# Early staging of the first batch and an even gMLP pace in a block-sparse attention + gMLP kernel

## The chip, the cores and the metric

The kernel runs on one core of one Trainium2 chip. The metric is the device time of one execution in microseconds (us); lower is better. The runs of the kernel before are summed up by their median. Engines are named as in the profile: PE (TensorE matmuls), PEld (TensorE weight loads), DVE (VectorE), ACT (ScalarE), POOL (GpSimd) and SP (SyncE, which here only issues DMAs). L12 is line 12 of the kernel before.

## What is computed

Two stages in one launch. First, attention with a block mask: batch 4, 8 heads, 768 positions, head dimension 64, blocks of 32, so 24 x 24 blocks. A block pair is visible if the blocks are neighbours, if one is the first or last block, or if it is one of three sampled blocks of that row. Second, a gMLP with a spatial gate on the attention output of all heads side by side (512 features).

```python
scores = (1/8) * q @ k.T ;  scores = where(mask, scores, -1e9)
x = softmax(scores) @ v                      # heads side by side: (4, 768, 512)
h = relu(x @ w_in)                           # 512 -> 1024
u, v = h[..., :512], h[..., 512:]
v_n = (v - mean(v)) / sqrt(var(v) + 1e-6)    # over features
v_s = w_spatial @ v_n + b_spatial            # over positions, 768 x 768
out = (u * v_s) @ w_out                      # 512 -> 512
```

## The kernel before, in words

Heads are taken in pairs: pair p is heads 2p and 2p+1 of the running count, four pairs a batch, sixteen in all (NP). For each pair q, k and v are loaded in float32 into staging tiles (`st_tile`, L89; two buffers for each of q, k, v), cast to bf16 (`cast_qk` L104, `cast_v` L112, `prepare` L117, mostly on POOL), and q and k are transposed, so that a head's 64 features lie on partitions: by TensorE through PSUM for the first pairs (`tr_head` L227, `tr_pair` L236), by DMA transposes for later ones (`tr_dma` L264, then `split_pair` L269 copies the two heads to their places).

The mask is part of the score product. Rows 64 to 87 of a head's k tile (`kt`) hold an indicator of the key's block, and the same rows of its q tile (`qt`) hold a penalty for each block, so the matmul with 88 contraction rows adds the mask. The 24 x 24 matrix behind it (`allowed`, then `bm`) is built at the start by POOL's iota and selects (L189 to L198) and DVE (L205 to L216). The mask rows are the same for all heads: head 0's are made first, heads 1 to 3 get them by DVE copies (`mask_rows`, L530), heads 4 to 7 by two DMAs (L538).

The work is ordered by slots written out by hand, one exponential a slot. The first batch has 48 slots of half heads (`qk_exp_half` L308, loop at L561): first the first 384 query positions of all eight heads, three slots a head, then the second 384. A slot has a pair of score matmuls, one exponential of 128 x 768 on ACT, six matmuls with V for a slot LAG0 = 4 back (`av_half`), and what the loop adds: transposes of later pairs (`tr_slots`), and from slot 31 gMLP matmuls of the first batch, sixteen in all, two a slot in slots 31 to 34 and 43 to 46 (L600). `xtr_half` (L349) transposes the normalized attention output of a pair to give the gMLP its input `xt`. From slot 48 on there are twelve slots a pair (L605); from slot 55 the gMLP matmuls of a finished batch are spread evenly over the slots of the next one, by a budget (L631). The last batch's gMLP stands alone at the end.

A batch's gMLP is a list of 108 matmuls (`moe_units`, L407): twelve input products of four matmuls each (v0 to v5 for the half that is normalized, u0 to u5 for the other), six spatial products of six, and six output products of four. Each product's PSUM result is evacuated by DVE or ACT (`v_post`, `u_post`); after v2 and v5 POOL makes the reciprocal deviation of three chunks (L448), and `normalize` (L453) writes the normalized chunk `vn`, which the spatial products read. These products and the transposes take turns in two PSUM buffers with the tag "moe".

Each engine executes its instructions in program order, and so does SP's queue of DMA issues. The framework puts in the waits: an instruction waits for its data and, where it writes a buffer, for the readers of what was in it. So a load on SP that waits for a staging buffer holds up all loads behind it.

The gMLP weights are loaded in nine pieces through the buffers that the gMLP will use for its own intermediates (tags un, vsb, vn, gn; `load_weights`, L141) and cast by POOL (`cast_weights`).

Of the kernel before, what the change touches and what calls it, by code (L numbers as in the profile page):

```python
# [26 lines left out]
def kernel(  # L27
# [60 lines left out]

    def st_tile(p, nm):  # L89
        st[nm, p] = work.tile([128, 2, NCH * D], FP32, tag=f"st_{nm}", bufs=2, name=f"st_{nm}")  # L90
        return st[nm, p]
# [47 lines left out]
    w_tags = deque(["un", "vsb", "vn", "gn"])  # L139

    def load_weights(n):  # L141
        for _ in range(n):
            src, dst = w_pieces.popleft()
            a, f = src.shape[1:]
            t = work.tile([128, NCH * DH // 2], FP32, tag=w_tags[0], bufs=2,
                          name="wst")[:, 0:a * f].rearrange("p (a f) -> p a f", a=a)
            w_tags.rotate(-1)
            nc.sync.dma_start(out=t, in_=src)
            if len(dst.shape) == 4:
                t = t.rearrange("p a (s c) -> p a c s", c=NCH)  # L150
            w_staged.append((t, dst))
# [7 lines left out]
    stq, stk = st_tile(0, "q"), st_tile(0, "k")  # L159
    nc.scalar.dma_start(out=stk[:, 0:1], in_=dram(k, 0, 0, 1))  # L160
    nc.scalar.dma_start(out=stk[:, 1:2], in_=dram(k, 0, 1, 1))
    nc.sync.dma_start(out=samp_i, in_=_listify(sampled_blocks).bitcast(I32))
    for h in range(2):
        nc.sync.dma_start(out=stq[:, h:h + 1], in_=dram(q, 0, h, 1))
    load(1, "kq")
    load(0, "v")

# [5 lines left out]
    nc.vector.memset(allowed, 0.0)  # L173
    nc.vector.memset(ind_nat, 0.0)
# [12 lines left out]

    colidx = const.tile([NB, NB], FP32)
    nc.gpsimd.iota(colidx, pattern=[[1, NB]], base=0, channel_multiplier=0,  # L189
                   allow_small_or_imprecise_dtypes=True)  # L190
    for c in (-1, 0, 1):
        nc.gpsimd.affine_select(out=allowed, in_=allowed, compare_op=ALU.not_equal,
                                fill=1.0, base=c, pattern=[[1, NB]], channel_multiplier=-1)
    for c in (0, NB - 1):
        nc.gpsimd.affine_select(out=allowed, in_=allowed, compare_op=ALU.not_equal,
                                fill=1.0, base=-c, pattern=[[0, NB]], channel_multiplier=1)
    nc.gpsimd.affine_select(out=ind_nat, in_=ind_nat, compare_op=ALU.not_equal, fill=1.0,
                            base=0, pattern=[[-1, NB], [0, BLK]], channel_multiplier=1)  # L198
    make_identity(nc, ident)

# [3 lines left out]

    nc.vector.memset(allowed[:, 0:1], 1.0)  # L205
    nc.vector.memset(allowed[:, NB - 1:NB], 1.0)
    nat_tile(0, "q"), nat_tile(0, "k")
    samp_f = const.tile([NB, 2 * NR], FP32)
    nc.vector.tensor_copy(out=samp_f, in_=samp_i)
    for r in range(NR):  # L210
# [8 lines left out]
    nc.scalar.activation(out=ind, in_=ind_nat.rearrange("b (p c) -> b c p", c=NCH),  # L219
                         func=AF.Copy)  # L220
# [5 lines left out]

    def tr_head(h, nm, copy):  # L227
        ps = psum.tile([128, S], BF16, tag="moe", bufs=2)
        for c in range(NCH):
            nc.tensor.transpose(out=ps[0:D, c * 128:(c + 1) * 128], in_=nat[nm, 0][:, c, h],  # L230
                                identity=ident)
        copy((qt if nm == "q" else kt)[h][0:D, :], ps[0:D, :])
# [3 lines left out]
    def tr_pair(p, nm, third):  # L236
        if third == 0:
            tr_ps[nm] = psum.tile([128, S], BF16, tag="moe", bufs=2, name="ps_tr")
        src, ps = nat[nm, p], tr_ps[nm]
        for c in (2 * third, 2 * third + 1):  # L240
            nc.tensor.transpose(out=ps[:, c * 128:(c + 1) * 128],
                                in_=src[:, c].rearrange("p h d -> p (h d)"), identity=ident)
        if third == 2:
            nat.pop((nm, p))
            for h in range(2):
                nc.vector.tensor_copy(out=(qt if nm == "q" else kt)[(2 * p + h) % H][0:D, :],  # L246
                                      in_=ps[h * D:(h + 1) * D, :])

    tr_head(0, "k", dve_copy)
    nc.vector.tensor_copy(out=kt[0][D:KR, :], in_=ind)  # L250
    keep_warm(4, 128)
# [6 lines left out]
    keep_warm(2, 128)  # L258
    tr_head(0, "q", dve_copy)
    keep_warm(8, 128)  # L260
# [88 lines left out]
    def xtr_half(p, grp):  # L349
        if grp == 0:  # L350
            xt_ref[p] = work.tile([128, S], BF16, tag="xt", bufs=8, name="xt")
        ps = psum.tile([128, S], BF16, tag="moe", bufs=2, name="ps_x")
        xn = xn_ref.pop(("half", p))
        for c in range(NCH // 2):
            nc.tensor.transpose(out=ps[:, c * 128:(c + 1) * 128], in_=xn[:, c], identity=ident)
        nc.vector.tensor_copy(out=xt_ref[p][:, grp * HALF:(grp + 1) * HALF], in_=ps[:, 0:HALF])
# [11 lines left out]
    def xtr_third(p, third):  # L368
        if third == 0:
            xt_ref[p] = work.tile([128, S], BF16, tag="xt", bufs=8, name="xt")  # L370
            tr_ps["x"] = psum.tile([128, S], BF16, tag="moe" if p < NP - 1 else "sc", bufs=2,
                                   name="ps_x")
        ps = tr_ps["x"]
        for c in (2 * third, 2 * third + 1):
            nc.tensor.transpose(out=ps[:, c * 128:(c + 1) * 128], in_=xn_ref[p][:, c],
                                identity=ident)
        if third == 2:
            xn_ref.pop(p)
            nc.vector.tensor_copy(out=xt_ref[p], in_=ps)
# [19 lines left out]
    def moe_ps(last):  # L399
        if not last:  # L400
            return psum.tile([128, 512], FP32, tag="moe", bufs=2, name="ps_moe")
        tail_tags.rotate(-1)
        if tail_tags[0] == "sc":
            return psum.tile([128, 1024], FP32, tag="sc", bufs=2, name="ps_sc")[:, 0:512]
        return psum.tile([128, 512], FP32, tag=tail_tags[0], bufs=2, name="ps_t")

    def moe_units(b):  # L407
# [13 lines left out]

        def add(n, operands, post):
# [4 lines left out]
            def step(i):  # L427
                if i == 0:
# [3 lines left out]
                                 start=(i == 0), stop=(i == n - 1))  # L432
                if i == n - 1:
                    post(box[0])
            units.extend((lambda i=i: step(i)) for i in range(n))

        def v_post(tcc, ps):
# [8 lines left out]
            if tcc % 3 == 2:  # L446
# [4 lines left out]
                                        in1=mhalf[:, cs], op=ALU.pow)  # L451

# [6 lines left out]
        def u_post(tcc, ps):  # L459
            nc.scalar.activation(out=un[:, tcc, :], in_=ps, func=AF.Relu)  # L460
            if tcc > 0:
                normalize(tcc - 1)
            if tcc == NCH - 1:
                normalize(tcc)

        def in_proj(tcc, cols, post):
# [3 lines left out]
        order = ("v0 v1 u0 v2 u1 u2 v3 v4 u3 v5 u4 u5" if b == 0 else  # L470
                 "v0 v1 v2 v3 v4 v5 u0 u1 u2 u3 u4 u5" if last else
                 "v0 v1 u0 v2 u1 v3 u2 v4 u3 v5 u4 u5")
# [6 lines left out]
        def g_tr(tcc):  # L479
            ps = psum.tile([128, S], BF16, tag="moe", bufs=2, name="ps_g")  # L480
# [42 lines left out]
    LAG0 = 4  # L523
    N0 = H * NCH

    cast_qk(0, "k", slice(1, 2), nc.vector)
    cast_qk(0, "q", slice(1, 2), nc.scalar)
    prepare(1, "kq")
    cast_v(0)
    def mask_rows(h):  # L530
        for t in (kt, qt):
            nc.vector.tensor_copy(out=t[h][D:KR, :], in_=t[0][D:KR, :])

    mask_rows(1)
    load(2, "kq")
    load(1, "v")
    for t in (kt_all, qt_all):
        nc.sync.dma_start(out=t[D:KR, 4:H, :],  # L538
                          in_=t[D:KR, 0:1, :].to_broadcast([NB, H - 4, S]))
    load(3, "kq")  # L540
    load(2, "v")
    load_weights(2)
    load(3, "v")
    load_weights(2)
    nc.sync.dma_start(out=b_col, in_=moe_b_spatial.rearrange("(p c) -> p c", c=NCH))

    tr_slots = {}
    for p, slots in ((1, (2, 2, 2, 3, 3, 3)), (2, (7, 8, 8, 9, 10, 10)),
                     (3, (13, 14, 14, 15, 16, 16)), (4, (36, 37, 38, 39, 40, 41))):
# [3 lines left out]
    def first_batch_rest(g):  # L553
        if LAG0 <= g < N0 + LAG0:
            av_half(g - LAG0)
        for grp in range(2):
            p, r = divmod(g - 11 - grp * N0 // 2, NCH)
            if r == 0 and 0 <= p < NG:
                xtr_half(p, grp)

    for g in range(N0):  # L561
# [7 lines left out]
        if g in (1, 4):  # L569
            mask_rows(2 if g == 1 else 3)  # L570
        if g == 3:
            prepare(2, "kq")
            cast_v(1)
        if g == 8:
            prepare(3, "kq")
            cast_v(2)
            cast_v(3)
            load(4, "kqv")
            load_weights(3)
        if g == 18:  # L580
            cast_weights(4)
            prepare(4, "kq")
            load(5, "kq")
        if g == 34:
            prepare(4, "v")
            load(5, "v")
            cast_weights(2)
        if g == 38:
            prepare(5, "kq")
            cast_weights(1)  # L590
        if g == 43:
            load(6, "kq")
            prepare(5, "v")
            load(6, "v")
        if g == 45:
            wspt(0)
            wspt(1)
        if g == 30:
            moe_q.extend(moe_units(0))
        if g in (31, 32, 33, 34, 43, 44, 45, 46):  # L600
            moe_q.popleft()()
# [3 lines left out]
    for p in range(NG, NP + 1):  # L605
        for s in range(12):
# [6 lines left out]
            if p == NG:  # L613
                if s < 6:
                    tr_pair(p + 1, "kq"[s // 3], s % 3)
            elif p + 1 < NP and s in (5, 9):
                split_pair(p + 1, "k" if s == 5 else "q")
# [25 lines left out]
            if p == NG and s in (2, 3, 6, 7):  # L643
                wspt((2, 3, 6, 7).index(s) + 2)
# [40 lines left out]
```

## Time and profile before

| | |
|---|---|
| median of 13 runs | 225.21 us (223.83 to 227.68) |
| the profiled execution | 224.38 us, of which the span in the profile is 222.3 us |
| granted TensorE clock | 0.997 |
| exponentials, first batch (L322) | 48, mean 814 ns |
| exponentials, later batches (L287) | 144, mean 813 ns |
| POOL casts of k (L110) | 15, mean 848 ns |
| POOL's longest wait for a load of k | 16.5 us; 41.3 us in seven waits |
| loads of k on SP, issue to landing | median 4.9 us |
| input read and output written | 24.38 MB and 6.29 MB |

A row of the chain of work gives start, duration and what ran; it follows the last instruction back to what released it. A row of the timeline gives start, duration, engine, line, operation, what it writes and reads, and how many like it are merged. A mean duration of overlapping instructions is longer than the pitch at which they follow each other, so pitches are taken from starts or from merged rows.

### The profile page before, as it was taken

Reading aid. Unit: us, or ns where it says so; the run is one execution under the profiler, and the core shown is the slowest. Engines: PE = TensorE matmul, PEld = TensorE weight load, DVE = VectorE, ACT = ScalarE, POOL = GpSimd, SP = SyncE. Lnnn points to the kernel's source line nnn. Section 1 sums busy time; section 2 is a strip of 40 time slices with the busy share of each in tenths; the row PEclk is TensorE's granted clock in tenths of the full one; section 3 lists DMA queues with packets and bytes.
Section 4 is the critical chain, followed back from the end, with each engine's and each line's share of the span. In section 5 each row is a group of like instructions: output and inputs, shape, how many; then the busy total and the mean of one; then the engine's idle time right before and its main releaser. Section 6 shows DMA issues by size and latency. Waiting matters only on the chain.

```text
span 222.3 us, 5351 instructions
## 1 busy us (share of the span) xinstructions
PE 213.5 (96%) x2154; PEld 128.6 (58%) x2154; DVE 132.3 (60%) x301; ACT 178.2 (80%) x247; POOL 64.5 (29%) x89
## 2 busy tenths in 40 slices
PE   7998999999999999999998999999999999999992
PEld 3676666675666666666564565655666655544540
DVE  5886438573777434367877645276877433684441
ACT  5698999999999889989988688888899885275351
POOL 5444646995036040400609100400602000022000
PEclk9999999999999999999999999999999999999998
DMA  6799999999951498999672289999150324620015
GB/s 207 249 248 379 386 414 375 199 140 263 312 157 39 99 227 208 261 328 283 193 191 101 59 123 233 130 291 283 24 106 3 59 50 83 209 104 0 0 72 212
DMA packets 56308, 40.55 MB, mean 182 GB/s; under 512 B 39324, under 2 KB 51804, under 8 KB 56284
## 3 DMA queue, kind: packets, MB, share of 16 engines
q1 hardware_dynamic: 55996, 39.83, 68.8%
q10 hardware_dynamic: 288, 0.39, 0.6%
q8 instruction: 16, 0.26, 0.5%
q14 instruction: 8, 0.07, 0.1%
HBM read 24.38 MB, written 6.29 MB: 138 GB/s over the span
## 4 chain that ended last, share of the span: by engine, by line
PE 78%; DMA 8%; DVE 6%; ACT 5%; issue 1%; POOL 1%; SPq 1%; POOLq 0%; DVEq 0%; ACTq 0%
PE ps_moe L431 27%; PE ps L283 17%; PE ps_av L299 10%; PE ps_t L431 7%; PE ps L318 5%; DMA st_k<-in_k_dram 5%; PE ps_sc L431 3%; DMA tt_k<-nat_k 3%; ACT a_all L322 3%; PE ps_av L334 2%; PE wps L182 2%; ACT a_all L287 2%; DVE kt_all L272 1%; DVE vn L454 1%; PE ps L230 1%
## 5 line engine op out<-in xcount | busy, mean ns | idle before, releaser
L287 ACT ACTIVATE a_all<-ps 128x768 bf16<-128x768 f32 x144 | 114.3, 813 | 16.4 <-PE ps L283 8.3
L283 PE MATMUL ps<-qt_all,kt_all 88*128 88x384 bf16 x288 | 70.3, 325 | 0.3 <-ACT a_all L287 0.2
L299 PEld LDWEIGHTS <-a_all 128*128 128x128 bf16 x864 | 46.1, 97 | 35.0 <-issue 1.1
L299 PE MATMUL ps_av<-vv,a_all 128*128 128x65 bf16 x864 | 50.8, 194 | 0.0
L431 PE MATMUL ps_moe<-w_in_t,xt 128*128 128x512 bf16 x144 | 42.7, 378 | 0.0
L322 ACT ACTIVATE a_all<-ps 128x768 bf16<-128x768 f32 x48 | 35.8, 814 | 2.7 <-PE ps L318 1.7
L431 PE MATMUL ps_moe<-vn,w_spt 128*128 128x512 bf16 x108 | 32.5, 378 | 1.3 <-DVE vn L454 1.3
L431 PEld LDWEIGHTS <-xt 128*128 128x128 bf16 x192 | 18.4, 97 | 16.2 <-DVE qt_all L246 0.6
L448 POOL TENSOR_SCALAR std<-mv 128x3 f32<-128x3 f32 x8 | 2.0, 246 | 83.0 <-DVE mv L445 82.9
L110 POOL CAST nat_k<-st_k 128x768 bf16<-128x768 f32 x15 | 12.7, 848 | 41.3 <-DMA st_k<-in_k_dram 41.3
L318 PE MATMUL ps<-qt_all,kt_all 88*128 88x384 bf16 x96 | 23.4, 324 | 0.8 <-ACT a_all L322 0.2
L489 DVE SCALAR_TENSOR_TENSOR gn<-ps_moe,b_col,un 128x512 bf16<-128x512 f32 x18 | 13.5, 748 | 15.3 <-PE ps_moe L431 15.3
L431 PE MATMUL ps_moe<-w_out_t,gt 128*128 128x512 bf16 x72 | 21.1, 378 | 0.1
L431 PEld LDWEIGHTS <-w_spt 128*128 128x128 bf16 x144 | 13.7, 97 | 11.6 <-issue 1.1
L283 PEld LDWEIGHTS <-kt_all 88*128 88x128 bf16 x288 | 19.3, 98 | 0.9 <-issue 0.7
L444 DVE BATCH_NORM_STATS2 stats<-vsb 128x6 f32<-128x512 bf16 x24 | 16.7, 695 | 1.4 <-ACT vsb L439 0.8
L334 PEld LDWEIGHTS <-a_all 128*128 128x128 bf16 x288 | 14.7, 98 | 4.8 <-issue 0.3
L441 DVE TENSOR_SCALAR vsb<-ps_moe 128x512 bf16<-128x512 f32 x18 | 12.4, 689 | 8.3 <-PE ps_moe L431 8.2
L334 PE MATMUL ps_av<-vv,a_all 128*128 128x65 bf16 x288 | 17.0, 194 | 0.1
L113 POOL CAST vv<-st_v 128x768 bf16<-128x768 f32 x16 | 13.7, 857 | 8.3 <-PE ps_av L334 4.6
L454 DVE TENSOR_SCALAR vn<-vsb,mv,rstd 128x512 bf16<-128x512 bf16 x24 | 12.9, 567 | 5.0 <-POOL rstd L450 4.9
L365 DVE TENSOR_TENSOR xn<-ps_av,rc 128x384 bf16<-128x384 f32 x24 | 13.4, 557 | 0.8
(91 smaller groups left out, 220.9 us busy)
## 6 DMA issues: line engine op xcount, KB each, us to landing
st_v<-in_v_dram SPq DMA_DIRECT2D x16, 384.0 KB, 6.4
out_dram<-osb SPq DMA_DIRECT2D x24, 256.0 KB, 2.5
st_k<-in_k_dram SPq DMA_DIRECT2D x15, 384.0 KB, 4.9
st_q<-in_q_dram SPq DMA_DIRECT2D x15, 384.0 KB, 3.9
wst<-in_moe_w_spatial_dram SPq DMA_DIRECT2D x3, 768.0 KB, 9.5
wst<-in_moe_w_in_dram SPq DMA_DIRECT2D x4, 512.0 KB, 8.3
wst<-in_moe_w_out_dram SPq DMA_DIRECT2D x2, 512.0 KB, 7.9
st_k<-in_k_dram ACTq DMA_DIRECT2D x2, 192.0 KB, 2.6
```

The costliest lines, as they stand in the source:

```text
L113: nc.gpsimd.tensor_copy(out=vv[p % NG][:, :, :, 0:D], in_=st.pop(("v", p)).rearrange("p h (c d) -> p h c d", d=D))
L283: nc.tensor.matmul(out=ps[:, hf * 512:hf * 512 + HALF], lhsT=kt[j % H][:, ci * 128:(ci + 1) * 128], rhs=qt[j % H][:, hf * HALF:(hf + 1) * ...
L287: nc.scalar.activation(out=a_ref[j][:, ci, :].rearrange("p (b c) -> p b c", b=2), in_=ps.rearrange("p (b c) -> p b c", b=2)[:, :, 0:HALF], ...
L299: nc.tensor.matmul(out=av_ref[j][:, qc, :], lhsT=a_ref[j][:, ci, qc * 128:(qc + 1) * 128], rhs=vv[p % NG][:, h, ci, :], start=(ci == 0), s ...
L318: nc.tensor.matmul(out=ps[:, u * 512:u * 512 + HALF], lhsT=kt[j][:, ci * 128:(ci + 1) * 128], rhs=qt[j][:, grp * HALF:(grp + 1) * HALF], s ...
L322: nc.scalar.activation(out=a_ref["half", gh][:, 2 * i:2 * i + 2, :], in_=ps.rearrange("p (b c) -> p b c", b=2)[:, :, 0:HALF], func=AF.Exp, ...
L334: nc.tensor.matmul(out=av_ref["half", gh][:, qc, :], lhsT=a_ref["half", gh][:, ci, qc * 128:(qc + 1) * 128], rhs=vv[p][:, h, ci, :], start ...
L365: nc.vector.tensor_tensor(out=xn_ref[p][:, :, h, :], in0=ps[:, :, 0:D], in1=rc.to_broadcast([128, NCH, D]), op=ALU.mult)
L431: nc.tensor.matmul(out=box[0], lhsT=lhs, rhs=rhs, start=(i == 0), stop=(i == n - 1))
L444: nc.vector.bn_stats(out=stats, in_=vsb[:, tcc, :])
L454: nc.vector.tensor_scalar(out=vn[:, tcc, :], in0=vsb[:, tcc, :], scalar1=mv[:, tcc, 0:1], scalar2=rstd[:, tcc:tcc + 1], op0=ALU.subtract, ...
L489: nc.vector.scalar_tensor_tensor(out=gn[:, tcc, :], in0=ps, scalar=b_col[:, tcc:tcc + 1], in1=un[:, tcc, :], op0=ALU.add, op1=ALU.mult)
```

## The change

- Staging: pairs 2 and 3 of the first batch no longer wait for the two staging buffers. k2 with q2, k3 with q3, and v2 with v3 are loaded into three of the gMLP's buffers (`stage_two`). The order of loads on the queues changes with it: the first head's q goes to ACT's queue, pair 2 directly behind v0, the mask DMAs between the loads, then the rest.
- Preparation: POOL's casts of the first batch, of pair 4 and of four weight pieces are queued in one list ahead of the slot loop. The second head's casts move from DVE and ACT to POOL.
- Mask: `allowed` is computed by DVE from two iotas (squared difference of block numbers at most 1, or edge row) in place of five POOL selects; the indicator is copied by DVE instead of ACT, and k's first mask rows by ACT instead of DVE. Six of the fourteen short warm-up matmuls between the first transposes go, and two behind them (eight become six). Mask rows of heads 2 and 3 are copied by one instruction for each of k and q; q's rows of heads 4 and 5 by DVE instead of DMA.
- Order: LAG0 becomes 6. Pairs 4 and 5 are transposed by DMA instead of TensorE, from slot 28 on in SP's queue, together with all six w_spatial transposes. The gMLP runs one matmul a slot from slot 29 (19 in all). k's split moves from step 5 to step 7 of a pair.
- gMLP: the two PSUM buffers are named, and a transpose of `xt` takes the one that is not in use without taking its turn. Normalizing is queued and spread; v5 comes before u3 in batches 1 to 3 (numbers 0 to 2). u0's relu in the first batch is on DVE.

```diff
+    def stage():
+        w_tags.rotate(-1)
+        return work.tile([128, NCH * DH // 2], FP32, tag=w_tags[-1], bufs=2, name="wst")
+    def stage_two(a, b):
+        t = stage().rearrange("p (u h x) -> p u h x", u=2, h=2)
+        st[a], st[b] = t[:, 0], t[:, 1]
...
+    stage_two(("k", 2), ("q", 2))
+    stage_two(("k", 3), ("q", 3))
+    stage_two(("v", 2), ("v", 3))
     nc.scalar.dma_start(out=stk[:, 0:1], in_=dram(k, 0, 0, 1))
-    nc.scalar.dma_start(out=stk[:, 1:2], in_=dram(k, 0, 1, 1))
+    nc.scalar.dma_start(out=stq[:, 0:1], in_=dram(q, 0, 0, 1))
     nc.sync.dma_start(out=samp_i, in_=_listify(sampled_blocks).bitcast(I32))
-    for h in range(2):
-        nc.sync.dma_start(out=stq[:, h:h + 1], in_=dram(q, 0, h, 1))
+    nc.sync.dma_start(out=stk[:, 1:2], in_=dram(k, 0, 1, 1))
+    nc.sync.dma_start(out=stq[:, 1:2], in_=dram(q, 0, 1, 1))
     load(1, "kq")
     load(0, "v")
+    load(2, "kq")
...
+    nc.vector.tensor_copy(out=ind, in_=ind_nat.rearrange("b (p c) -> b c p", c=NCH))
+    nc.vector.scalar_tensor_tensor(out=edge, in0=row, scalar=float(NB - 1), in1=row,
+                                   op0=ALU.subtract, op1=ALU.mult)
+    nc.vector.tensor_scalar(out=edge, in0=edge, scalar1=0.0, scalar2=None, op0=ALU.is_equal)
+    nc.vector.tensor_tensor(out=diff, in0=diff, in1=diff, op=ALU.mult)
+    nc.vector.tensor_scalar(out=allowed, in0=diff, scalar1=1.0, scalar2=edge,
+                            op0=ALU.is_le, op1=ALU.max)
...
     tr_head(0, "k", dve_copy)
-    nc.vector.tensor_copy(out=kt[0][D:KR, :], in_=ind)
-    keep_warm(4, 128)
+    act_copy(kt[0][D:KR, :], ind)
...
-    keep_warm(2, 128)
     tr_head(0, "q", dve_copy)
-    keep_warm(8, 128)
+    keep_warm(6, 128)
...
+    moe_bank = [0]
+    def bank(shape, dtype, turn=True):
+        b = 1 - moe_bank[0]
+        if turn:
+            moe_bank[0] = b
+        return psum.tile(shape, dtype, tag=f"moe{b}", bufs=1, name="ps_moe")
...
+        norm_q = deque()
+        products = [0]
+        def normalize_next():
+            if norm_q and norm_q[0][1] <= products[0]:
+                normalize(norm_q.popleft()[0])
...
+                if i == n // 2:
+                    normalize_next()
                 if i == n - 1:
                     post(box[0])
+                    products[0] += 1
...
+                norm_q.extend((i, products[0] + 2) for i in range(tcc - 2, tcc + 1))
...
-            if tcc > 0:
-                normalize(tcc - 1)
-            if tcc == NCH - 1:
-                normalize(tcc)
+            normalize_next()
...
-        order = ("v0 v1 u0 v2 u1 u2 v3 v4 u3 v5 u4 u5" if b == 0 else
+        order = ("v0 v1 u0 v2 u1 u2 v3 v4 v5 u3 u4 u5" if b == 0 else
                  "v0 v1 v2 v3 v4 v5 u0 u1 u2 u3 u4 u5" if last else
-                 "v0 v1 u0 v2 u1 v3 u2 v4 u3 v5 u4 u5")
+                 "v0 v1 u0 v2 u1 v3 u2 v4 v5 u3 u4 u5")
...
-    LAG0 = 4
+    LAG0 = 6
...
-    cast_qk(0, "k", slice(1, 2), nc.vector)
-    cast_qk(0, "q", slice(1, 2), nc.scalar)
+    cast_qk(0, "k", slice(1, 2), nc.gpsimd)
+    cast_qk(0, "q", slice(1, 2), nc.gpsimd)
     prepare(1, "kq")
     cast_v(0)
...
+    mask_rows("k", 1, 2)
+    mask_rows("q", 1, 2)
+    mask_dma("k", 4, H)
     load(1, "v")
...
     load(3, "kq")
+    mask_dma("q", 6, H)
     load(2, "v")
-    load_weights(2)
     load(3, "v")
-    load_weights(2)
+    load_weights(NDM)
+    load(4, "kq")
     nc.sync.dma_start(out=b_col, in_=moe_b_spatial.rearrange("(p c) -> p c", c=NCH))
+    prepare(2, "kq")
+    cast_v(1)
+    prepare(3, "kq")
+    cast_v(2)
+    cast_v(3)
+    cast_weights(NDM)
+    prepare(4, "kq")
+    load_weights(3)
...
-    for p, slots in ((1, (2, 2, 2, 3, 3, 3)), (2, (7, 8, 8, 9, 10, 10)),
-                     (3, (13, 14, 14, 15, 16, 16)), (4, (36, 37, 38, 39, 40, 41))):
+    for p, slots in ((1, (2, 2, 2, 3, 4, 4)), (2, (7, 7, 8, 9, 9, 10)),
+                     (3, (13, 13, 14, 15, 15, 16))):
...
+    xtr_slots = {13: (0, 0), 19: (1, 0), 25: (2, 0), 31: (3, 0),
+                 38: (0, 1), 46: (1, 1), 50: (2, 1), 56: (3, 1)}
...
+        if g == 1:
+            mask_rows("k", 2, 4)
+            mask_rows("q", 2, 4)
+        if g == 5:
+            mask_rows("q", 4, 6)
+        if g == 28:
+            tr_dma(4, "k")
+            tr_dma(4, "q")
             cast_weights(2)
+            load(4, "v")
+            load(5, "kqv")
             wspt(0)
             wspt(1)
+            cast_weights(1)
+            prepare(5, "kq")
+            wspt(2)
+            wspt(3)
+            tr_dma(5, "k")
+            tr_dma(5, "q")
+            wspt(4)
+            wspt(5)
+            load(6)
             moe_q.extend(moe_units(0))
...
+        if g in (36, 42):
+            cast_v(4 if g == 36 else 5)
+        if g in (39, 45):
+            split_pair(4, "k" if g == 39 else "q")
+        if g >= 29:
             moe_q.popleft()()
...
-            elif p + 1 < NP and s in (5, 9):
-                split_pair(p + 1, "k" if s == 5 else "q")
+            if p + 1 < NP and s in (7, 9):
+                split_pair(p + 1, "k" if s == 7 else "q")
```

## The prediction

> **What bounds the kernel now.** I read the page's busy times first, then the chain of work that ended last, then TensorE's score matmuls one by one (they give the pitch of the slots), and last the waits.
>
> ```profile
> PE 213.5 (96%) x2154; PEld 128.6 (58%) x2154; DVE 132.3 (60%) x301; ACT 178.2 (80%) x247; POOL 64.5 (29%) x89
> ```
>
> TensorE looks full, but its ends are modelled, so 96% does not say that it had work all the time. What each piece costs on it is seen in the chain, where pieces follow without a gap:
>
> ```profile
> 23.33 4.21 ACT a_all L322 x6
> ...
> 32.45 0.43 PE ps_moe L431 x2
> 32.88 0.19 PE ps_av L334 x6
> 33.07 0.33 PE ps L318 x2
> ...
> 36.45 0.17 PE ps_x L355 x3
> ...
> 36.94 0.11 PE ps_tr L241 x2
> ```
>
> So on TensorE a slot's score pair costs 0.33, its attention-times-V 0.19, one gMLP matmul 0.43/2 = 0.216, a transpose 0.055; on ScalarE one exponential costs 4.21/6 = 0.702. A first-batch slot without gMLP work needs 0.52 of TensorE and 0.702 of ScalarE: ScalarE bounds it. With one gMLP matmul TensorE needs 0.736, with two 0.95, and TensorE bounds it. From slot 55 (51.0 us) to 186 us TensorE's pieces join without a gap save one, so there only TensorE work removed, or that one gap, counts.
>
> How far the first 48 slots are from their bound is read from the starts of the score pairs (slots 0, 6, 20, 29, 48, 55 start at 7.79, 12.90, 24.20, 30.56, 46.00, 50.96). The largest step between two, slots 13 and 14:
>
> ```profile
> 18.14 0.48 PE L318 MATMUL ps<-qt_all,kt_all 88*128 88x384 bf16 x2
> 19.74 0.49 PE L318 MATMUL ps<-qt_all,kt_all 88*128 88x384 bf16 x2
> ```
>
> and what stands behind it in the chain, a load of keys that was issued only when the staging buffer came free:
>
> ```profile
> 11.62 6.77 DMA st_k<-in_k_dram
> ...
> 18.54 0.84 POOL nat_k L110
> ...
> 19.43 0.28 PE ps_tr L241 x2
> ```
>
> Slots 0 to 48 take 38.21 against 48 x 0.702 = 33.7 of ScalarE: 4.5 us of TensorE's and ScalarE's time are lost here. The one later loss is TensorE's wait for the normalized v (121 to 123 us, second batch):
>
> ```profile
> PE ps_moe L431 <- DVE vn L454: 1.3, 2, 0.9
> ```
>
> **The change, part by part** (gains positive, against the profiled execution: span 222.3, 2.08 outside it, 224.38; the median of the 13 runs, 225.21, lies 0.83 above it).
>
> *Start-up.* TensorE runs eight warm-up matmuls to 4.77, transposes to 5.55, four warm-ups to 6.06 (0.51), the mask product to 6.48, two warm-ups to 6.69 (0.21), the transposes of q, then a copy (0.55) and the first scores at 7.79. The six warm-ups go: up to 0.72. VectorE's new list is longer: the copy of ind, five small operations for band and edge (0.17 to 0.29 each, from the rows of L215 and L211, about 1.1), then the old list. The copy of ind reads every sixth element. The nearest rows are the same copy on ScalarE, 1.22, and a dense 24x768 copy on VectorE, 0.35. [...] I take 0.7. POOL drops five selects (0.72 + 0.46); the one that ind waits for took 0.99 and now comes first, done near 2.4; so the mask matrix is ready about 2.4 + 0.7 + 1.1 + 0.15 + 0.87 + 0.17 = 5.4 (4.70 before), still ahead of the mask product at 5.55. With ind at 1.22 it would be 5.9 and cost 0.35. Moving half of the mask copies and casts to ScalarE and POOL hides in ScalarE's idle 1.57 before L225 and POOL's 2.69. Gain **0.55** (0.2 to 0.72).
>
> *Slots 0 to 6.* Slot 6 needs heads 2 and 3 and waited for VectorE's copy of q at 12.90; VectorE sets this stretch (4.44 of 5 us busy, 10 to 15). There the new order puts two-head mask copies ahead of the copies of pair 1: 0.55 each instead of 0.35, so +0.4 before slot 6. These rows speak against it:
>
> ```profile
> 8.03 0.90 DVE L532 COPY kt_all<-kt_all 24x768 bf16<-24x768 bf16 x1
> 8.86 0.34 DVE L532 COPY qt_all<-qt_all 24x768 bf16<-24x768 bf16 x1
> ```
>
> The first ran beside a POOL cast (7.90 to 8.73) and took 0.55 more; the second did not. [...] By the rows, two following copies share one wait, and a copy also goes first. I take 0.05 beyond the 0.4: **-0.45** (-1.65 to 0).
>
> *Slots 6 to 20.* 11.30 for 14 slots. k, q of pairs 2 and 3 and v get buffers of their own, so SP issues k2 and q2 at about 3.6 to 4.5 instead of 7.74 and 8.76, and pair 3 at about 7 instead of 11.6. Do the transfers come sooner, or only queue sooner? In the 5 us stretches to 20 us the queues moved 193, 253, 260 and 321 GB/s: 3.5 MB by 15 us. What stands before k3 is now 3.5 MB and a mask copy, no weights; so even at those rates k3 lands near 15.5, and its cast precedes slot 13 (about 17.5). New waits: SP waits for ScalarE's mask rows (near 5 and 7 us) with v1, k3, q3, v2, v3 and the weights behind it; the DMA engines have k1, q1, v0, k2, q2 to carry meanwhile. POOL's casts of pair 2 wait for head 1's transposes (near 9), with v1 and pair 3 behind. V starts two slots later (LAG0 6), at slot 6; free while ScalarE bounds (0.52 < 0.702), and in slots 52 and 53 too. Without the stall the pitch lies between 0.702 and the 0.743 of slots 14 to 20: 14 x 0.73 = 10.2. Gain **1.1** (0.3 to 1.5).
>
> *Slots 20 to 29.* At ScalarE's pitch before and after: 0.
>
> *Slots 29 to 48.* Before 15.44, with 16 gMLP matmuls in eight slots of 0.95 and 12 transposes of pair 4. After: 19 x 0.736 + three transposing slots x 0.17 = 14.5, and 0.1 for gMLP matmul 3 (slot 32), which reads what slot 31 transposed. Gain **0.85** (0.5 to 1.1). Moved here: pairs 4 and 5 go to DMA transposes (SP issue 1.2 to 1.9, landing 3.6 to 3.9), and all six w_spatial transposes (5.1); ten in SP's queue from slot 28, about 15 us, with loads 5 and 6 among and behind them. Pair 4 is due at slot 48, 15 us later; load 6 at slot 58. Hidden; uncovered, each landing costs 4 to 6. The four PSUM copies of a pair (0.555) become SBUF copies (0.34, or 0.89 beside a cast), in VectorE's slack. u0's relu to VectorE and the bank rule: 0.
>
> *Slots 48 to 55.* ScalarE's pitch; pair 5's removed transposes (0.11 a slot) were under it: 0.
>
> *From slot 55.* Three gMLP matmuls fewer, 3 x 0.216 = 0.65, less three transposes now at slot 56, 0.17. Gain **0.48**. v5 is moved ahead of u3 and the normalizing spread over u4 and u5; in the second batch that brings its last statistics four matmuls, near 1.8 us, earlier than the 1.3 wait. I take **1.1** (0 to 1.3): the copies of normalized v still meet POOL casts. The splits of k at step 7 instead of 5 lie under gapless TensorE.
>
> Sum: 0.55 - 0.45 + 1.1 + 0.85 + 0.48 + 1.1 = 3.63. Profiled 220.75, median 225.21 - 3.63 = **221.6**.
>
> **The rivals.**
> A, as above: chance 0.5.
> [...] Chance 0.2.
> C, everything falls to its bound: 0.72 + 0 + 1.5 + 1.1 + 0.48 + 1.3 = 5.1: 220.1. Chance 0.12.
> D, the gain stays out: the stall at pair 3 turns into slower early slots (slots 0 to 6 at -1.65, 6 to 20 at 0.3) and the normalized v is late again: 0.55 - 1.65 + 0.3 + 0.85 + 0.48 = 0.5: 224.7. Chance 0.08.
> E, slower: TensorE issues in order, so a gMLP matmul in slot 29 whose w_in isn't there stops attention too. Seven MB (first batch, w_in) must be cast by about 30 us. At the rates above they land by 25 and the last cast ends at 29. Each us beyond is lost, and it exceeds the gain once the mean rate after 5 us falls under some 225 GB/s; at 200 (the 220 GB/s seen from 14 to 17 us, and mask copies on 24 partitions) they land at 35, 5 us late: 226.5. Against: fewer mask bytes, 390 GB/s from 20 us. Chance 0.10.
>
> **How the numbers follow.** The terms' upper ends sum to 5.1, 220.1; their lower ends to -0.2, but all of them together is less likely than D (224.7). So 220.0 to 225.0, which leaves out E and the edges. This kernel's measurement tells a change from none at about 0.5% (1.1 us; faster is below 224.1): faster A, B, C 0.82; same D 0.08; slower E 0.10.
>
> **What would show it.** First scores near 7.2; slot 6 at 12.8 (B: over 13.5); no 1.6 us step at slot 14, slot 20 near 23; slots 29 to 48 at an even 0.74; slot 55 near 49; no wait of TensorE for the normalized v. Wrong if TensorE waits for w_in or a DMA transpose, or slots 0 to 20 take as long as before.

## The result and the profile after

The changed kernel takes 222.41 us (median of 11 runs, 222.05 to 224.32), the kernel before 225.26 (48 runs): ratio 0.9894, interval 0.987 to 0.9918. On a second occasion the changed kernel took 222.44, ratio 0.9882 (0.9847 to 0.9917). The ratios leave out runs that lie more than 1.5% above the fastest of their kernel. The forecast was 221.6 in a range of 220.0 to 225.0: faster, as said, with 2.85 us between the medians instead of 3.63.

Line numbers in the rows below are those of the profiled kernel itself. The busy times, as before, say little (changed kernel, first profile):

```profile
PE 213.0 (96%) x2122; PEld 127.7 (58%) x2122; DVE 136.1 (61%) x302; ACT 177.1 (80%) x245; POOL 66.8 (30%) x89
```

TensorE has 32 matmuls and transposes fewer and is as full. This execution (223.68, span 221.9) misleads, because it is 1.3 above the kernel's own median. TensorE's rows of the timeline (start, duration, line, operation) show why. First this profile:

```profile
6.27 0.85 PE L262 MATMUL ps_moe<-ident,nat_q 128*64 128x128 bf16 x6
...
7.85 0.80 PE L348 MATMUL ps<-qt_all,kt_all 88*128 88x384 bf16 x2
...
9.58 0.65 PE L348 MATMUL ps<-qt_all,kt_all 88*128 88x384 bf16 x2
...
10.72 0.50 PE L348 MATMUL ps<-qt_all,kt_all 88*128 88x384 bf16 x2
```

The same instructions in a second profile of the same kernel (222.15, span 220.4):

```profile
6.12 0.52 PE L262 MATMUL ps_moe<-ident,nat_q 128*64 128x128 bf16 x6
...
7.38 0.48 PE L348 MATMUL ps<-qt_all,kt_all 88*128 88x384 bf16 x2 [0.29 <-DVE qt_all L244]
...
8.36 0.50 PE L348 MATMUL ps<-qt_all,kt_all 88*128 88x384 bf16 x2
...
9.36 0.50 PE L348 MATMUL ps<-qt_all,kt_all 88*128 88x384 bf16 x2
```

Six transposes take 0.85 in one and 0.52 in the other, a score pair 0.80 and 0.48. These two durations are what is called half pace and full pace below: in the first profile TensorE worked at half pace until about 9.9 us, in the second at full pace from about 5.7. The profile of the kernel before (full pace near 6) is therefore compared with the second one. The stages, by the starts of the score pairs:

| stage | before | changed, 2nd profile | gain | forecast |
|---|---|---|---|---|
| first scores | 7.79 | 7.38 | 0.41 | 0.55 |
| slots 0 to 6 | 5.11 | 5.66 | -0.55 | -0.45 |
| slots 6 to 20 | 11.30 | 10.19 | 1.11 | 1.1 |
| slots 20 to 29 | 6.36 | 6.36 | 0 | 0 |
| slots 29 to 48 | 15.44 | 14.82 | 0.62 | 0.85 |
| slots 48 to 55 | 4.96 | 5.29 | -0.33 | 0 |
| slot 55 to the last matmul | 167.29 | 166.93 | 0.36 | 1.58 |
| sum | | | 1.62 | 3.63 |

The other 0.61 of the 2.23 between these two executions (224.38 and 222.15) lie behind the last matmul and outside the span. From the last matmul to the end of the span it is 4.05 in all three profiles built on the kernel before and 3.75 to 3.77 in all eleven of the changed kernel and its variants, so 0.30 belongs to the change; its cause was not looked for. The time outside the span was 2.09 against 1.78 here, but 1.78 and 2.67 in the other two profiles built on the kernel before, so these 0.31 are spread.

The step of 1.6 at slot 14 is gone (changed kernel, second profile, starts of slots 13 and 14):

```profile
17.96 0.48 PE L348 MATMUL ps<-qt_all,kt_all 88*128 88x384 bf16 x2
...
18.87 0.49 PE L348 MATMUL ps<-qt_all,kt_all 88*128 88x384 bf16 x2
```

The wait for the normalized v is gone too. But in the list of waits (who, for whom, us in total, times, longest) another of the same size has taken its place:

```profile
PE ps_moe L472 <- DVE vsb L485: 1.3, 2, 0.7
```

### The profile page after: what moved, and what is told of

It is laid out like the page before. It is cut to its first block, busy times and chain, and to the rows that moved or that the text cites. A ratio compares the mean times of both kernels' runs of the same rounds, so it can differ in the third digit from the quotient of the medians.

```text
span 221.9 us, 5292 instructions
## 1 busy us (share of the span) xinstructions
PE 213.0 (96%) x2122; PEld 127.7 (58%) x2122; DVE 136.1 (61%) x302; ACT 177.1 (80%) x245; POOL 66.8 (30%) x89
## 4 chain that ended last, share of the span: by engine, by line
PE 83%; DVE 8%; ACT 5%; issue 1%; POOL 1%; ACTq 0%; POOLq 0%
PE ps_moe L472 32%; PE ps L313 18%; PE ps_av L329 11%; PE ps L348 7%; ACT a_all L317 4%; PE ps_t L472 4%; PE ps_sc L472 4%; PE ps_av L364 3%; PE wps L196 2%; DVE kt_all L278 1%; DVE kt_all L302 1%; PE ps_moe L262 1%; DVE vsb L485 1%; DVE vn L499 1%; DVE qt_all L278 1%
## 5 line engine op out<-in xcount | busy, mean ns | idle before, releaser
L472 PE MATMUL ps_moe<-w_in_t,xt 128*128 128x512 bf16 x160 | 48.8, 378 | 1.4 <-DVE vsb L485 1.3
L472 PE MATMUL ps_moe<-vn,w_spt 128*128 128x512 bf16 x120 | 35.4, 378 | 0.0
L535 DVE SCALAR_TENSOR_TENSOR gn<-ps_moe,b_col,un 128x512 bf16<-128x512 f32 x20 | 15.0, 750 | 17.1 <-PE ps_moe L472 16.9
L124 POOL CAST nat_k<-st_k 128x768 bf16<-128x768 f32 (+1 forms) x14 | 11.5, 821 | 40.3 <-DMA st_k<-in_k_dram 31.6
L472 PE MATMUL ps_moe<-w_out_t,gt 128*128 128x512 bf16 x80 | 23.1, 378 | 0.1
L555 DVE COPY osb<-ps_moe 128x512 f32<-128x512 f32 x10 | 6.9, 692 | 11.5 <-PE ps_moe L472 11.4
L395 DVE TENSOR_TENSOR xn<-ps_av,rc 128x384 bf16<-128x384 f32 x24 | 13.4, 557 | 0.8
```

Of the source, the lines that this page charges most:

```text
L395: nc.vector.tensor_tensor(out=xn_ref[p][:, :, h, :], in0=ps[:, :, 0:D], in1=rc.to_broadcast([128, NCH, D]), op=ALU.mult)
L472: nc.tensor.matmul(out=box[0], lhsT=lhs, rhs=rhs, start=(i == 0), stop=(i == n - 1))
L535: nc.vector.scalar_tensor_tensor(out=gn[:, tcc, :], in0=ps, scalar=b_col[:, tcc:tcc + 1], in1=un[:, tcc, :], op0=ALU.add, op1=ALU.mult)
```

## The experiments

Theory after the result: staging and pace did what was forecast; the shortfall lies after slot 55, where one wait replaced another, because k's split now stands ahead of the copy of v on VectorE. Rival: the moment at which TensorE reaches full pace decides, and the removed warm-ups moved it. Unless said otherwise a run is the changed kernel with one edit, compared with its 222.44. Warm-ups put back, normalizing undone and ordinary staging were timed on the same occasion as that 222.44. The others were timed on other chips, each beside the kernel before; for them the ratio to the kernel before counts as well, against 0.9882 for the changed kernel.

**The changed kernel again.** No edit.

> The changed kernel once more, for a second profile and a tighter interval. In its first profile TensorE ran at half pace until 9.9 us (the six transposes of q took 0.78 us, not 0.45), where the kernel before reached full pace near 6, and the profiled execution (223.68) was 1.3 us above its own median (222.41). Theory 1 (the start-up depends on when the clock opens, which differs between executions): this profile can show another moment of full pace, and where it comes by 7 us, slot 6 starts near 13 and the time is near 222.2. Theory 2 (fewer warm-up matmuls always leave TensorE at half pace until about 10 us): the same 0.78 us rows again, slot 6 at 14.6. Time 222 to 223 either way.

The median was 222.44, with all six runs between 222.15 and 222.59; full pace came near 5.7 and slot 6 at 13.04. That is theory 1: the moment is not the kernel's alone.

**Warm-ups put back.**

```diff
     act_copy(kt[0][D:KR, :], ind)
+    keep_warm(4, 128)
...
+    keep_warm(2, 128)
     tr_head(0, "q", dve_copy)
-    keep_warm(6, 128)
+    keep_warm(8, 128)
```

> The changed kernel with the eight removed short warm-up matmuls put back. Theory 1: full pace still comes at a moment that differs between executions; the time is that of the changed kernel or up to 0.7 us more (the removed warm-ups' own time). Theory 2: full pace by 6 to 7 us as in the kernel before; slots 0 to 6 take about 5.3 instead of 6.75 us; 1 us or more faster than the changed kernel, 221.4 or less.

The median was 222.63 (221.92 to 223.44). The first scores came at 8.05, 0.67 later than 7.38, of which slots 0 to 6 (5.49) give 0.17 back. There is no gain of 1 us, so theory 2 falls. The rival is not excluded in a weaker form: a start at half pace until 9.8 us or later shows in three of the ten profiles without the short warm-ups and in none of the four that have them (this one and the three with the start-up of the kernel before). So few cannot tell whether the removed warm-ups make such a start more frequent.

**Twice the warm-up.** `keep_warm(16, 512)` for `keep_warm(8, 512)`.

> The changed kernel with sixteen instead of eight warm-up matmuls of 512 columns at the start. Theory: TensorE reaches full pace after a busy stretch whose end differs between executions (4.5, 5.5 to 6 and 9.9 us so far), and that makes the two groups of times of the changed kernel (222.05 to 222.6, and 223.2 to 224.3). With steady matmuls to 6.5 us or more full pace always comes during the warm-ups: the first scores are 1.0 to 2.0 us later, the median 223.2 to 224.2, and all executions lie within 0.8 us. Rival: the two groups have another cause (loads); then they stay apart by 1.2 us or more here too.

The median was 223.95 (223.19 to 224.64), and the first scores came at 9.07, at full pace (0.52 for six transposes at 6.94). The median is as expected. The spread of 1.45 is not under 0.8, and the runs do not fall into two groups either, so the run decides nothing about what causes the groups.

**Normalizing undone.**

```diff
-                if i == n // 2:
-                    normalize_next()
...
-            normalize_next()
+            if tcc > 0:
+                normalize(tcc - 1)
+            if tcc == NCH - 1:
+                normalize(tcc)
...
-        order = ("v0 v1 u0 v2 u1 u2 v3 v4 v5 u3 u4 u5" if b == 0 else
+        order = ("v0 v1 u0 v2 u1 u2 v3 v4 u3 v5 u4 u5" if b == 0 else
...
-                 "v0 v1 u0 v2 u1 v3 u2 v4 v5 u3 u4 u5")
+                 "v0 v1 u0 v2 u1 v3 u2 v4 u3 v5 u4 u5")
```

> The changed kernel with the order of v5 and u3 and the normalizing of the kernel before. My prediction counted 1.1 us for this part. If it holds, this run is 1.1 us slower (223.5) and TensorE waits again for the normalized v. Rival, after the changed kernel's profile: the wait for the normalized v (1.3) has only become a wait for the copy of v out of PSUM (1.3, twice in the second and third batch), so this run is within 0.4 us of the changed kernel.

The median was 223.07 (222.41 to 225.22, 18 runs), 0.63 slower. Slot 55 to the last matmul took 167.35, 0.42 more than with the new order, with a wait for the copy of v of 1.4. That is nearly the rival: beside the moved split this part brings 0.4 in its stage, not 1.1.

**Split at step 5.**

```diff
-            if p + 1 < NP and s in (7, 9):
-                split_pair(p + 1, "k" if s == 7 else "q")
+            if p + 1 < NP and s in (5, 9):
+                split_pair(p + 1, "k" if s == 5 else "q")
```

> The changed kernel with k split at step 5 of a pair again, not step 7. In the changed kernel TensorE waits 1.3 us in two places (second and third batch) for the copy of v out of PSUM, which stands on VectorE behind the normalizing and the two split copies of k at 0.89 each, beside POOL's casts. If the moved split makes this wait, it goes and the time falls by about 1 us (221.3). Rival: the split only meets another piece of the new order; a wait of 1 to 1.5 us is seen elsewhere and the time stays within 0.3 us.

The median was 220.97 (220.53 to 222.38), the ratio to the kernel before 0.9787 (0.9728 to 0.9846). Slot 55 to the last matmul took 165.29, 1.64 less. Here is VectorE's timeline in the second batch, first in the changed kernel (second profile), with the POOL cast beside the copies and the matmul of TensorE that waited:

```profile
106.01 0.90 DVE L499 TENSOR_SCALAR vn<-vsb,mv,rstd 128x512 bf16<-128x512 bf16 x1 [1.32 <-POOL rstd L494]
...
107.52 1.24 DVE L302 COPY kt_all<-tt_k 64x768 bf16<-64x768 bf16 x2
107.54 1.02 POOL L127 CAST vv<-st_v 128x768 bf16<-128x768 f32 x1
...
108.69 0.67 DVE L485 TENSOR_SCALAR vsb<-ps_moe 128x512 bf16<-128x512 f32 x1
...
109.41 0.38 PE L472 MATMUL ps_moe<-w_in_t,xt 128*128 128x512 bf16 x1 [0.69 <-DVE vsb L485]
```

Then with the split at step 5:

```profile
105.19 0.69 DVE L302 COPY kt_all<-tt_k 64x768 bf16<-64x768 bf16 x2
106.66 0.90 DVE L499 TENSOR_SCALAR vn<-vsb,mv,rstd 128x512 bf16<-128x512 bf16 x1 [0.78 <-POOL rstd L494]
107.48 0.18 DVE L394 RECIPROCAL rc<-ps_av 128x6 f32<-128x6 f32 x1
107.70 0.56 DVE L395 TENSOR_TENSOR xn<-ps_av,rc 128x384 bf16<-128x384 f32 x1
108.17 0.68 DVE L485 TENSOR_SCALAR vsb<-ps_moe 128x512 bf16<-128x512 f32 x1
```

At step 5 the two copies take 0.69, in a gap in which VectorE waits for POOL's deviation anyway. At step 7 they stand between the normalizing and the copy of v, beside POOL's casts, and take 1.24; TensorE's next product waits 0.69 for the PSUM buffer that the copy of v frees. With the split at step 5 no wait of TensorE over 0.3 is left after slot 55.

**Normalizing alone.** The kernel before with only the queue of normalizing and v5 ahead of u3 (the reverse of the diff two above, with the split at step 5).

> The kernel before with only the changed kernel's queue of normalizing and v5 ahead of u3; k's split stays at step 5. In the changed kernel undoing this part made no difference while the split stood at step 7. If the two hang together, this part alone takes away the wait for the normalized v (1.3 us) without putting another in its place: 1.0 to 1.4 us faster than the kernel before, as predicted for this term (1.1). Rival: a wait for the copy of v appears here too, and the time is within 0.4 us of the kernel before.

The median was 225.67, ratio 0.9998 (0.9957 to 1.0039), so the expected gain in the total did not show. Its profile lost 2.1 us in slots 6 to 20 (13.40), which this edit does not touch. But slot 55 to the last matmul took 165.82, 1.47 less than before, with no wait of TensorE over 0.3 there. In that stage the theory holds; in the total it isn't shown.

**Ordinary staging.** The three `stage_two` lines removed.

> The changed kernel with pairs 2 and 3 of the first batch staged in the two ordinary buffers again, so that their loads wait for the casts of pairs 0 and 1; all else is as in the changed kernel. My prediction counted 1.1 us for slots 6 to 20. If staging is what removed the stall, a wait of TensorE for k of pair 2 or 3 returns and the time rises by 1 to 3 us (the loads of v and the weights now wait behind as well). Rival: the order of the loads alone did it (no weights ahead of pair 3); then within 0.4 us of the changed kernel.

The median was 223.5 (16 runs: seven at 222.40 to 222.74, nine at 223.46 to 224.74). Slots 6 to 20 took 10.19, the same. So for the stage the rival's number holds: the extra buffers aren't needed to remove the stall. What removed it is the question of the next run. The profile had half pace until about 9.8 (slots 0 to 6 in 6.53). Why more of its runs are late isn't settled.

**Ordinary staging, and the second head's casts on VectorE and ScalarE.** The edit above and

```diff
-    cast_qk(0, "k", slice(1, 2), nc.gpsimd)
-    cast_qk(0, "q", slice(1, 2), nc.gpsimd)
+    cast_qk(0, "k", slice(1, 2), nc.vector)
+    cast_qk(0, "q", slice(1, 2), nc.scalar)
```

> The changed kernel with the ordinary two staging buffers for pairs 2 and 3 and with the second head's casts on VectorE and ScalarE again. With the buffers alone undone the slots 6 to 20 still took 10.19 us, as with them. If that is because the second head's casts are now done by 4.1 to 6.3 us on POOL, and so free the buffers early, this run issues the load of k2 near 7.5 again and slots 6 to 20 take longer: 10.6 to 11.3, 0.4 us or more slower than with the buffers alone undone. Rival: the order on the queues (mask copies apart from each other, head 1's data first) is enough; 10.2 again.

The median was 223.52, the ratio 0.9882. Slots 6 to 20 take 11.79, so undoing both loses 1.6 there. Here are the issues of k2 in SP's timeline, staged ordinarily with POOL's casts, then with these casts:

```profile
4.64 0.37 SPq L110 DMA_DIRECT2D st_k<-in_k_dram  x1
```

```profile
8.79 0.37 SPq L110 DMA_DIRECT2D st_k<-in_k_dram  x1
```

The earlier casts are enough without the extra buffers: they free the ordinary ones 4.15 us sooner. Whether the extra buffers would be enough with the old casts was not run. The total does not show the expected loss: the median is that of the run with the buffers alone undone (223.5), whose profiled start was at half pace while this one's was not, and the ratio is that of the changed kernel. So only the stages are compared.

**Mask rows head by head.**

```diff
-        if g == 1:
-            mask_rows("k", 2, 4)
-            mask_rows("q", 2, 4)
+        if g in (1, 4):
+            mask_rows("k", 2 + g // 4, 3 + g // 4)
+            mask_rows("q", 2 + g // 4, 3 + g // 4)
```

> The changed kernel with the mask rows of heads 2 and 3 copied head by head as in the kernel before (head 2's in slot 1, head 3's in slot 4, behind the copies of pair 1). With full pace by 6 us the changed kernel takes 5.5 to 5.66 us for slots 0 to 6, before 5.11. My theory (the two-head copies ahead of pair 1's copies, and their waits for POOL's casts, hold slot 6): slots 0 to 6 take 5.1 to 5.3 and the time falls by 0.3 to 0.5 us. Rival: the copies of slots 0 to 4 are paced by the transposes, and head 3's copies now collide with a cast later; no change (within 0.2).

The median was 222.34 (221.64 to 223.39), not to be told from 222.44; the expected 0.3 to 0.5 does not show in the total. Slots 0 to 6 took 5.13 instead of 5.66 (5.49 to 6.13 in the other profiles with two-head copies and full pace), slots 6 to 20 took 10.35 instead of 10.19; that leaves 0.37 by slot 20. VectorE's copies in slot 1, in the changed kernel (second profile) and here:

```profile
10.05 0.72 DVE L574 COPY kt_all<-kt_all 24x1536 bf16<-24x1536 bf16 x1
10.69 0.54 DVE L574 COPY qt_all<-qt_all 24x1536 bf16<-24x1536 bf16 x1
```

```profile
10.08 0.39 DVE L574 COPY kt_all<-kt_all 24x768 bf16<-24x768 bf16 x1
10.39 0.34 DVE L574 COPY qt_all<-qt_all 24x768 bf16<-24x768 bf16 x1
```

**Pace undone.**

```diff
-        if g >= 29:
+        if g in (31, 32, 33, 34, 43, 44, 45, 46):
             moe_q.popleft()()
+            moe_q.popleft()()
```

> The changed kernel with the gMLP matmuls of the first 48 slots as in the kernel before: sixteen, two a slot in slots 31 to 34 and 43 to 46, in place of nineteen, one a slot. Prediction: slots 29 to 48 take 15.4 or, without the twelve transposes of pair 4, about 14.9 us, and three matmuls of 0.216 go to the stage after slot 55: 0.65 to 1.2 us slower (223.1 to 223.6). Rival: ScalarE's queue evens it out, slots 29 to 48 at 14.5 (eight slots of 0.95 and eleven of 0.70 are 15.3, but TensorE can run ahead by two slots); then only the 0.65, or less.

The median was 223.58 (222.99 to 224.29), 1.14 above 222.44; by the ratios (0.9911 against 0.9882) it is 0.65, and their intervals overlap. The stages are clearer: slots 29 to 48 take 15.55, 0.73 more, and the stage after slot 55 takes 0.27 more. This is within what was expected, and running ahead does not even it out. The three moved matmuls alone would be 0.65 in the last stage; why it shows only 0.27 isn't settled.

**Split and mask rows together.**

> The changed kernel with k's split at step 5 again (alone: 220.97, no wait left for the copy of v) and the mask rows of heads 2 and 3 copied head by head (alone: slots 0 to 6 in 5.13 us instead of 5.5 to 6.07, 0.16 given back in slots 6 to 20). The two lie in different stages, so my theory has them add up: 220.6 (220.3 to 220.9), slots 0 to 6 near 5.1, no wait of TensorE over 0.7 us after slot 55. Rival: the gain at slot 6 is lost again before slot 48, 221.0.

The median was 221.1 (219.93 to 222.98, six runs), the ratio to the kernel before 0.9807 (0.9747 to 0.9866). Its profiled execution was the 222.98, with score pairs at half pace (0.80 to 0.85) in slots 0 to 3; slot 55 to the last matmul took 165.27. That the two gains add up is not shown. The split alone has the lowest median and ratio seen, and its interval (to 0.9846) just clears that of the changed kernel's second measurement (from 0.9847); the interval of this run overlaps both.

**The kernel before again.**

> The kernel before once more, for a second profile. In its first profile full pace of TensorE came near 6 us and the time was 224.38, 0.9 under its median. Theory 1 (the moment of full pace differs between executions of one kernel): the profile may show another moment; the later it is, the later slot 6, and the time of the profiled execution follows it. If full pace comes near 6 again, slots 0, 6, 20, 29, 48 start within 0.3 us of 7.79, 12.90, 24.20, 30.56, 46.00. Rival: before's spread comes from its loads; then slots 0 to 6 are the same and slot 14 or 20 moves.

The median was 225.73. Its profiled execution took 228.41 with a granted clock of 0.981, so its stages stay out of the comparison above. By itself it shows what the rival named: full pace came near 6.5 and slots 0 to 6 took 5.10, as in the first profile (5.11), but slots 6 to 20 took 15.20: the four score pairs that start from 21.55 to 25.52 us took 0.83 each, where the one at 19.31 took 0.48 and the one at 27.40 took 0.49.

## Why the prediction was right, and where it failed

*Right.* **Slots 6 to 20**: 1.11 for 1.1, by the stall that was named. But the extra buffers were not needed for it: with the ordinary ones the stage is 10.19 as well, since the casts moved to POOL free these in time. **Slots 0 to 6**: -0.55 for -0.45, by the step named: two-head copies of 0.72 and 0.54 ahead of pair 1's, where single ones took 0.39 and 0.34. The size differs between profiles: others with these copies at full pace took 5.49 to 6.13, which is -0.4 to -1.0. No run shows the -1.65 at the lower end of this term, which rival D's sum uses too. The two-head copy of k, 0.72 here, took 1.14 in the split run, with slots 0 to 6 in 6.07 and slot 6 at 13.63. Otherwise a slot 6 over 13.5, the mark of rival B, appears only with half pace (14.33 to 15.53) and with the warm-ups put back (13.54) or doubled (14.77). **Pace**: undone, it costs 0.73 + 0.27 = 1.00 in the two stages; the forecast for both its terms was 0.85 + 0.48. One item in it was too small. I counted 0.1 for gMLP matmul 3, which reads what slot 31 transposed. It waits for VectorE's copy of that, and slot 32 took 1.04 instead of 0.74, so 0.3 (changed kernel, second profile, slots 32 and 33):

```profile
31.96 0.49 PE L348 MATMUL ps<-qt_all,kt_all 88*128 88x384 bf16 x2
...
32.58 0.39 PE L472 MATMUL ps_moe<-w_in_t,xt 128*128 128x512 bf16 x1
...
33.00 0.49 PE L348 MATMUL ps<-qt_all,kt_all 88*128 88x384 bf16 x2
```

w_in came in time (rival E out).

*Right by its number, but only at this moment of full pace.* **Start**: the copy of ind took 0.66 (changed kernel, first profile) for 0.7, and the first scores came 0.41 earlier for 0.55. No row of the kernel before shows that 0.7; it was my estimate between the 1.22 and the 0.35 of the nearest rows. But the mask matrix was ready near 5.65, not 5.4, and not ahead of the mask product. Where full pace comes by 4.5 us, that is the longer path. In the run with normalizing undone, which has the changed start, TensorE waits 0.66 for the mask matrix:

```profile
5.68 0.49 PE L285 MATMUL mq<-ind,bm 24*24 24x384 bf16 x2 [0.66 <-DVE bm L238]
...
7.36 0.48 PE L348 MATMUL ps<-qt_all,kt_all 88*128 88x384 bf16 x2 [0.29 <-DVE qt_all L244]
```

In the run with normalizing alone, which has the start of the kernel before and full pace as early, the first scores come 0.28 sooner:

```profile
5.28 0.49 PE L254 MATMUL mq<-ind,bm 24*24 24x384 bf16 x2
...
7.08 0.50 PE L318 MATMUL ps<-qt_all,kt_all 88*128 88x384 bf16 x2
```

*Failed.* One zero: "The splits of k at step 7 instead of 5 lie under gapless TensorE." The work on TensorE was gapless before, but on VectorE the moved copies (107.52 to 108.76 in the rows above) come in program order ahead of the copy of v (108.69) that TensorE awaits: 1.64 us. The term for the normalized v (1.1, to 1.3) was right by itself: 1.47 less in that stage with the split left at step 5. The run with all but the split (165.29) is 0.53 below that one (165.82), where the forecast for the rest of this stage was 0.48. Added up, 1.47 + 0.53 - 1.64 = 0.36, which is the 0.36 measured for a forecast of 1.58. I named what the split might cost in its own slots and not what is queued behind it.

A second zero, slots 48 to 55, measured -0.33. ScalarE's first exponential of slot 48 starts 0.35 after the one before it ends, although its scores are ready (changed kernel, second profile):

```profile
41.79 3.19 ACT L352 ACTIVATE a_all<-ps 128x768 bf16<-128x768 f32 x4
...
44.41 0.50 PE L313 MATMUL ps<-qt_all,kt_all 88*128 88x384 bf16 x2
...
45.32 2.21 ACT L317 ACTIVATE a_all<-ps 128x768 bf16<-128x768 f32 x3 [0.35 <-ACT a_all L352]
```

These slots took 5.27 to 5.29 in all profiles of the changed kernel and its variants but one: with buffers and casts undone they took 4.97. The cause stays open.

*Luck in the number.* Up to the last matmul 1.62 of the forecast 3.63 came, less than half. That the medians differ by 2.85 owes 0.61 to what lies behind the last matmul and outside the span, and 0.62 to the spread of the runs: the kernel before's median lies 0.88 above its profiled execution, the changed kernel's 0.26. The forecast had no term for either.

*Not foreseen.* The medians differ by 2.85, the matched profiles by 2.23. The stall of the kernel before can be worse than in its profile. The kernel with only the normalizing changed has the same first 31 slots; here is TensorE in its slots 10, 11, 13 and 14 (timeline). Below it are the stretches from 16 to 22 us, where the granted clock (0.97, 0.50, 0.68) stands ahead of the DMA share and the GB/s:

```profile
16.05 0.49 PE L318 MATMUL ps<-qt_all,kt_all 88*128 88x384 bf16 x2
...
17.92 0.49 PE L334 MATMUL ps_av<-vv,a_all 128*128 128x65 bf16 x6 [1.16 <-POOL vv L113]
18.22 0.83 PE L318 MATMUL ps<-qt_all,kt_all 88*128 88x384 bf16 x2
...
20.48 0.83 PE L318 MATMUL ps<-qt_all,kt_all 88*128 88x384 bf16 x2
...
21.51 0.49 PE L318 MATMUL ps<-qt_all,kt_all 88*128 88x384 bf16 x2
```

```profile
16.00:18.00 2.00, 0.84 (x15) 0.58 (x12) 1.62 (x4) 0.85 (x2) 0.83 (x1) 0.97 1.09 213
18.00:20.00 2.00, 2.00 (x19) 1.46 (x19) 0.26 (x1) 0.81 (x1) 0.12 (x1) 0.50 1.06 335
20.00:22.00 2.00, 2.00 (x23) 1.39 (x21) 0.63 (x3) 1.46 (x2) 1.65 (x3) 0.68 1.04 401
```

After waits for late q and v the score pair takes 0.83 until about 21 us. Slots 6 to 20 took 11.3, 13.4 and 15.2 in the three profiles of that code, and 10.19 or 10.20 in all seven profiles that have the changed kernel's staging, casts and mask copies; in those seven no score pair from slot 6 to 30 us took more than 0.50. But this drop of the clock is not most of the remaining 0.6. Of the 72 runs of the kernel before that the ratios of the three later occasions leave in, nine have a granted clock under 0.995, with a median of 227.15; the other 63 still have 225.56, 1.2 above the 224.38 of the profile. What else lifts them stays open.

## What to carry to other kernels

An instruction that is moved can cost what is queued behind it on its engine at the new place (1.64 us here), even where the engine that bounds the kernel has no gap: look for the next output that the bounding engine awaits. A load that is held up can be freed in two ways (a buffer more, an earlier cast), and here undoing one of them cost nothing in the stage while undoing both cost 1.6; so undo them together before crediting one. Compare profiles of executions in which TensorE reaches full pace at the same moment (it came near 5.7 and at 9.9 us in one and the same kernel here), and take a second profile when one is off its median.

## What the runs showed of the hardware

The first matmul starts at 1.17 us of the span (first profiles of both kernels). With the same first eight warm-ups, full pace came by about 4.5 us, between 5.7 and 6.5, near 9.8, and once near 14 (5.7 and 9.9 in one and the same kernel). The late cases took 0.9 to 2.4 us longer in slots 0 to 6 (6.53 and 6.75 against 5.66, 7.49 against 5.13 where the mask rows were copied head by head). The spread, from 3.3 to 13 us after the first matmul, is wide, and no run shows why the late starts are late.

The drop of the clock within an execution lasted, by the three rows above and if it went to 0.50 and back, (0.03 x 2 + 0.50 x 2 + 0.32 x 2) / 0.5 = 3.4 us, an estimate. In the second profile of the kernel before the score pairs at 19.83 and 26.80 took 0.55 and 0.57 and the four between them 0.83, so I estimate some 7 us there. In the first case TensorE was not idle ahead of the drop: it was busy for 1.72 of the 3.4 us before it (14.5 to 17.9), with no wait over 1.16. The granted clock of the profile reads 1.00 in the changed kernel's first profile from 6 to 10 us, while six transposes take 0.85; so the half pace of a start has to be read from the durations.

VectorE's copies between SBUF tiles and its normalizing took longer where they began while a POOL cast was under way. In the fourteen profiles 218 mask copies of 24x768, split copies of 64x768 and normalizing instructions of 128x512 began while a cast had 0.5 us or more to run, and 217 of them took 0.72 to 1.02. In the first profiles of the two kernels there are 30 of these, with 0.72 to 0.97, and each ended 0.14 to 0.21 after the cast. With no cast under way the copies took 0.32 to 0.36 and the normalizing 0.38 to 0.41.
